# Attention ahead of a mixture of experts: scores made once, normalised exponentials turned by DMA

## The chip, the cores and the metric

The kernel runs on one core of one Trainium2 chip, in one launch. The metric is the device time of that launch in microseconds (us), median of several executions. The engines are named as in the profile: PE is TensorE (matrix products; PEld its weight loads), DVE is VectorE, ACT is ScalarE, POOL is GpSimd, and SP is the engine from whose queue most DMAs are issued.

## What is computed

Four sequences of 576 tokens, eight heads of 64, go through rotary embedding, softmax attention, and then a mixture of eight experts with a Sinkhorn gate. Cut to what matters:

```
q_rot, k_rot = (rotate(q), rotate(k))
scores = scale * np.matmul(q_rot, k_rot.transpose(0, 1, 3, 2))
scores = scores - np.max(scores, axis=-1, keepdims=True)
attn = np.exp(scores)
attn = attn / (np.sum(attn, axis=-1, keepdims=True) + 1e-09)
attn_out = np.matmul(attn, v)
...
x = attn_out.transpose(0, 2, 1, 3).reshape(B * S, H * D)
P = np.exp(x @ w_gate - max)          # then 8 rounds of row and column scaling
for e in range(E):
    out += P[:, e:e+1] * (np.maximum(x @ w1[e], 0.0) @ w2[e])
```

## The kernel before, in words

**Precision.** All is fp32 at the ends. Most products split each operand into a high and a low f16 half ("hl", "hi" and "lo" in the names) and add three products: high x high, high x low, low x high.

**Pairs and units.** Two heads make a pair, 16 pairs in all, four to a sequence. The two heads of a pair stand in the upper and the lower 64 partitions, and their products run side by side on PE. Scores of a pair are made in nine units of 128 x 576 (two heads x 288), one PSUM tile (`s` or `t`, two banks) each.

**The attention before.** The scores are made twice. `s_mm` (L439) makes them with the queries on partitions, only to find each query's maximum (`most`, L462); `m_max` to `m_rows` (L474 to L506) bring the maxima into a row form R. `t_mm` (L508) makes the scores again with the keys on partitions, takes the maxima off by a product with `neg` (L522) and adds the three products (L526); `exps` (L534) writes the exponentials, `e_hi` (L538) and `e_lo` (L541) their f16 halves (tile `eb`). `av_mm` multiplies them with V (L562; in the first three pairs, p < WHOLE, in fp32 with one product, L556), and `sum_mm` (L576) sums the exponentials by products with ones. The sums then go through HBM and back in four steps of small DMAs (`sums_turn`, L586), are inverted on DVE, and `av_norm` and `x_half` (L620, L624) scale the result and split it into `xx`.

**Ahead of a pair** stand the load of Q and K (`load_qk`, L320), their maxima and scales (L294, L364), RoPE (products L386, sums L393) and the split into Z (L295 to L301). V is loaded once a sequence.

**The first expert** (expert 0: `f1_mm` L742, `f2_mm` L765, with ACT's and DVE's halves `hh` L758 and `hl` L763) is cut into five blocks of tokens. Three blocks may start while the attention runs, as soon as their tokens' `xx` is there, and fill PE; two come behind it, beside the gate (L981). After that the other experts run (`experts`, L1422; its products all have L1234).

**What sets the order.** `Plan` (L121) is a list scheduler in the program: each operation has engines, a duration from the table `US`, a due time (`AT`, `SH1`, `RANGES`), buffers that it takes, and what it depends on. Plan walks through time with these numbers and writes each engine's instructions out in that order. On the chip each engine works through its own list in order and waits for semaphores. The table's numbers make the order; they are no measurements.

Of the kernel before, what the change touches and what calls it, by code (L numbers as in the profile page):

```python
# [14 lines left out]
ALU = mybir.AluOpType  # L15
# [36 lines left out]
AT = dict(
    ld=-78.23, mx=-17.61, gm=-23.86, cq=-19.05, ck=-15.91, sc=-18.11, sq=-19.55, sk=-16.41, aq=-17.05, ak=-13.91,
    hq=-24.97, hk=14.53, lq=-34.5, lk=-23.36, mp=-11.68, mh=-11.58, ms=-11.53, ml=-11.48, mt=-10.98, mr=-10.78,
    vh=1.6, vl=-2.58, n0=16.63, d0=4.16, r0=6.82, x0=3.89, h0=4.69, l0=5.19, n1=21.63, d1=9.16, r1=11.82, x1=8.89,
    h1=9.69, l1=10.19,
)
AT_NEW = dict(ldv=-30.41, v0=-8.42, v1=-7.42, v2=-6.42, v3=-5.42, vg=-4.92, vr=-4.82, vp=-4.42)
AV_AT = ((3, 0, 0), (3, 0, 1), (4, 0, 2), (5, 0, 3), (6, 0, 4), (7, 1, 4), (8, 1, 0), (9, 1, 1), (10, 1, 2), (11, 1, 3))

SH1 = dict(
    mx=-0.35, T=0.09, vl=3.02, vh=-8.95, hq=-11.66, eh=-7.16, AVw=0.38, d00=-29.0, d01=-29.0, d02=-29.0, d03=-29.0,
    d10=-29.0, d11=-29.0, d12=-29.0, d13=-29.0, mp=-2.97, mh=-2.97, ms=-2.97, ml=-2.97, mt=-2.97, mr=-2.97,
    lk=-14.85, sc=-2.98, S=-0.04, M=-0.04, ex=-4.13, r0=15.28, r1=15.28, lq=-22.36, Q=-9.6, n0=18.1, n1=18.1,
    hk=-11.04, x0=-1.71, h0=-1.71, l0=-1.71, x1=-1.71, h1=-1.71, l1=-1.71, gm=-46.44, AV=2.25, ck=-0.18, sk=-0.18,
    ak=-0.18, ld=13.84, ldv=-6.05, el=-0.01, cq=-0.22, sq=-0.22, aq=-0.22,
# [3 lines left out]
    s=0.375, mx9=0.68, t=0.5, ex=0.73, eh=0.58, s8=0.42, t4=0.55, av=0.375, av32=1.03, q=0.62, mx=1.26, gm=0.08, tt=0.67, ptt=1.24, sc=0.72, hi=0.68, lo=0.74,  # L70
    ad=0.67, pro=1.37, m1=0.12, m2=0.25, mt=0.12, mr=0.8, n=0.6, d=2.4, dl=5.5, r=0.26, x=0.75, xd=0.37, xh=0.33, xl=0.7, xld=0.37,
# [1515 lines left out]
```

## Time and profile before

| | |
|---|---|
| median of three executions | 1700.3 us (1699.11 to 1700.4) |
| the profiled execution's own time | 1699.66 us |
| its span in the profile | 1697.9 us |
| busy: PE, DVE, ACT, POOL | 1640.5, 1365.7, 1089.8, 686.2 us |
| chain that ended last: PE, DVE, ACT | 85%, 6%, 3% |

A busy share is a mean over stages with different limits, so the stages have to be looked at one by one; and PE being busy does not mean that it runs at its best rate. The program has three stages: attention with most of three blocks of the first expert (to 440 us), gate and the rest of the first expert (to 530), the other experts (to the end).

### The profile page before, as it was taken

The page shows a single profiled execution, that of the slowest core. Times are in us where ns is not written, and L with a number is a line of the kernel's source. Part 1 is how long each engine was busy: PE and PEld are TensorE (multiplying, and loading weights), DVE is VectorE, ACT ScalarE, POOL GpSimd, SP SyncE. Part 2 cuts the span into 40 slices and gives each one's busy share as a digit, 9 for nine tenths or more (in the row PEclk, how much of TensorE's full clock was granted, in tenths as well). Part 3 has the DMA queues.
Part 4 walks back from the last instruction along what each step waited for, and adds up shares of the span by engine and source line. Part 5 has one row for each costly group of instructions (what it writes and reads, how often), then busy time and mean ns, then how long its engine had stood idle before and what let it go on. Part 6 is the DMA issues. An engine that isn't in the chain of part 4 may idle for free.

```text
span 1697.9 us, 39516 instructions
## 1 busy us (share of the span) xinstructions
PE 1640.5 (97%) x16098; PEld 1292.9 (76%) x16098; DVE 1365.7 (80%) x2629; ACT 1089.8 (64%) x2117; POOL 686.2 (40%) x595
## 2 busy tenths in 40 slices
PE   4898999999999999999999999999999999999998
PEld 2454445454455898989898998989898989898987
DVE  7988777752697988888888888888888878888877
ACT  3578777867237666666666666666666666666642
POOL 4466889876243333232323232332323233333310
PEclk8999999999999999999999999999999999999999
DMA  5242222200113464646455655556555555565543
GB/s 219 64 159 71 79 69 78 72 13 19 43 75 112 125 152 123 162 116 160 125 149 130 157 126 150 138 141 144 140 149 138 139 148 150 126 157 128 131 114 94
DMA packets 66543, 203.01 MB, mean 120 GB/s; under 512 B 14660, under 2 KB 19128, under 8 KB 62264
## 3 DMA queue, kind: packets, MB, share of 16 engines
q1 hardware_dynamic: 47640, 139.13, 24.2%
q0 software_dynamic: 18720, 61.35, 19.7%
q8 instruction: 126, 2.06, 0.5%
q14 instruction: 57, 0.47, 0.1%
HBM read 129.46 MB, written 9.64 MB: 82 GB/s over the span
## 4 chain that ended last, share of the span: by engine, by line
PE 85%; DVE 6%; ACT 3%; issue 2%; DMA 2%; POOL 1%; SPq 1%; POOLq 0%; DVEq 0%; ACTq 0%
PE m L1234 66%; PE g L752 4%; PE g L773 4%; PE av L562 3%; PE t L526 2%; PE s L459 2%; PE t L522 2%; DVE mraw L462 1%; PE as L576 1%; DVE Z L297 1%; DMA wraw<-in_w 1%; DVE raw L393 1%; ACT accA L1021 0%; PE av L556 0%; DVE vv L297 0%
## 5 line engine op out<-in xcount | busy, mean ns | idle before, releaser
L1234 PE MATMUL m<-w2h,h 128*128 128x256 f16 x3528 | 627.2, 273 | 3.3 <-DVE accB L1297 1.5
L1234 PEld LDWEIGHTS <-h 128*128 128x128 f16 x5292 | 515.3, 98 | 63.5 <-issue 2.0
L1234 PE MATMUL m<-w2l,h 128*128 128x256 f16 x1764 | 480.8, 273 | 0.0
L1234 PEld LDWEIGHTS <-w1h 128*128 128x128 f16 x3920 | 369.2, 98 | 40.0 <-issue 3.2
L1234 PE MATMUL m<-ts,w1h 128*128 128x256 f16 (+1 forms) x2240 | 347.6, 262 | 2.9 <-ACT m L1257 1.6
L1299 ACT ACTIVATE ev<-m,pp 128x256 f32<-128x256 f32 x468 | 197.5, 467 | 186.3 <-PE m L1234 185.3
L1234 PE MATMUL m<-ts,w1l 128*128 128x256 f16 (+1 forms) x1120 | 284.0, 262 | 0.0
L1234 PE MATMUL m<-xx,w1h 128*128 128x256 f16 (+1 forms) x1680 | 261.4, 262 | 0.0
L1184 POOL TENSOR_TENSOR wraw<-wraw 128x512 f32<-128x512 f32 x112 | 160.8, 1436 | 163.0 <-issue 141.0
L1279 POOL TENSOR_TENSOR h<-u,h 128x512 f16<-128x512 f32 (+1 forms) x70 | 78.2, 1117 | 358.1 <-ACT h L1275 341.0
L1234 PE MATMUL m<-xx,w1l 128*128 128x256 f16 (+1 forms) x840 | 213.1, 262 | 0.0
L1234 PEld LDWEIGHTS <-w1l 128*128 128x128 f16 x1960 | 191.8, 98 | 17.8
L1297 DVE SCALAR_TENSOR_TENSOR ev<-m,pp,ev 128x256 f32<-128x256 f32 x351 | 154.8, 478 | 45.3 <-ACT ev L1299 28.3
L541 POOL TENSOR_TENSOR eb<-e,eb 128x576 f16<-128x576 f32 x117 | 159.4, 1373 | 28.6 <-ACT eb L538 19.8
L462 DVE TENSOR_REDUCE mraw<-s 128x2 f32<-128x576 f32 x140 | 105.4, 753 | 59.4 <-PE s L459 58.3
L1275 ACT ACTIVATE h<-m 128x512 f16<-128x512 f32 (+1 forms) x210 | 120.4, 573 | 44.3 <-PE m L1234 40.8
L1260 DVE TENSOR_TENSOR u<-m,u 128x512 f32<-128x512 f32 (+1 forms) x140 | 88.9, 635 | 54.9 <-PE m L1234 29.2
L1275 ACT ACTIVATE h<-u 128x512 f16<-128x512 f32 (+1 forms) x210 | 122.3, 586 | 14.7 <-DVE u L1286 11.1
L534 ACT ACTIVATE e<-t,ebias,pc 128x576 f32<-128x576 f32 x117 | 97.1, 830 | 38.9 <-PE t L526 37.3
L1257 ACT COPY u<-m 128x512 f32<-128x512 f32 (+1 forms) x140 | 75.8, 542 | 71.5 <-PE m L1234 70.5
L1308 POOL DMA_DIRECT2D accA<-ev x78 | 69.0, 1019 | 126.4 <-ACT ev L1299 108.3
L1308 POOL DMA_DIRECT2D accB<-ev x52 | 45.1, 867 | 181.7 <-ACT h L1275 110.9
(177 smaller groups left out, 2800.2 us busy)
## 6 DMA issues: line engine op xcount, KB each, us to landing
ts<-xd SPq DMA_DIRECT2D x110, 512.0 KB
accA<-ev POOLq DMA_DIRECT2D x78, 512.0 KB, 6.1
wraw<-in_w SPq DMA_DIRECT2D x28, 1024.0 KB
raw<-in_qk SPq DMA_DIRECT2D x32, 576.0 KB
accB<-ev POOLq DMA_DIRECT2D x26, 512.0 KB, 7.2
ts<-xd SPq DMA_DIRECT2D x28, 256.0 KB
accB<-ev POOLq DMA_DIRECT2D x26, 256.0 KB, 3.2
vraw<-in_v SPq DMA_DIRECT2D x4, 1536.0 KB
```

The lines of the kernel that those rows point to most:

```text
L462: dve.reduce_max(o, ps[:, :, 0:HS], axis=AX.X)
L534: act.activation(e32, ps[:, :, 0:HS], AF.Exp, bias=ebias, scale=sc[p][0])
L541: engine[e].tensor_tensor(E[g][:, 1], e32, E[g][:, 0], op=ALU.subtract)
L1184: put(k, "pool", US["ptt"], lambda: pool.tensor_tensor(quad(o), quad(x), quad(y), op=op), deps, uses=[raw])
L1234: pe.matmul(live[bank][:, f_ * width : (f_ + 1) * width], step(x, i, f_), y[:, i], start=first and f_ == 0 and n == 0, stop=n == 5, skip_g ...
L1257: act.copy(live[n], live[src])
L1260: dve.tensor_tensor(live[n], live[x], live[n], **add)
L1275: act.activation(t[:, 0:cols], live[src], func)
L1279: engine[eng].tensor_tensor(l, live[src], h, **sub)
L1297: dve.scalar_tensor_tensor(o, x, s, o, op0=ALU.mult, op1=ALU.add)
L1299: act.activation(o, x, AF.Copy, scale=s)
L1308: pool.dma_start(out=a, in_=ev[th][:, 0:nt], accum_op=ALU.add)
```

## The change

The scores are made once, with the queries on partitions, in five steps a pair (four of 128 queries for each head, one of 64 queries for both heads together). Nine score tiles a pair result, in three PSUM buffers `s`. For each tile DVE takes the negated maximum (`m_max`); ACT makes the bias from it and the exponential in place, with the row's sum (`e_exp`); DVE inverts the sum (`e_inv`); ACT writes the normalised high half (`e_hi`), DVE the low half (`e_lo`), into one of six tiles `et`. SP then turns the tile by a DMA transposition (`e_turn`) into `ET`, where the keys are on partitions, and `av_mm` multiplies with V once five transpositions of a half are there. `ET` is held once for each half of the queries. The products with ones, the maxima's turn, the second score pass and the sums' way through HBM are gone; `x_half` reads PSUM and writes `xx`. RoPE's sums, the scaling of Q, K, V and of the first expert's weights and their low halves move to POOL (`choice`). For the first eight pairs (`SOLO`) the two heads' scores are separate steps. The V blocks shrink from six to five. The tables of due times are new, and RANGES is empty.

The diff, cut (before and after):

```diff
+def choice(pool_us, dve_us):
+    return (("pool", US[pool_us]), ("none", 0.0))[:1] + ((("dve", US[dve_us]),) if BOTH else ())
...
+    def s_mm(n, ps, js):
+        p, i = divmod(n, 5)
+        zz = Z[p]
+        for j in js[:1] if i == TAIL else js:
+            ps[j] = ps_s.tile([P, 2, 512], F32, tag="s", name="s")
+        for x, y in ((0, 2), (1, 2), (0, 3)):
+            for kh in range(2):
+                for j in js:
...
+                    pe.matmul(o, q, zz[r, y, QH[kh]], start=(x, y) == (0, 2), stop=(x, y) == (0, 3))
+    def m_max(ps, b):
+        b.append(small.tile([P, 1], F32, tag="nm", bufs=4, name="nm"))
+        dve.tensor_reduce(b[0], ps[:, :, 0:HS], axis=AX.XY, op=ALU.max, negate=True)
+    def e_exp(p, ps, b):
+        c = small.tile([P, 1], F32, tag="nb", bufs=4, name="nb")
+        act.activation(c, b[0], AF.Copy, bias=E_TOP * math.log(2.0), scale=sc[p][0])
+        b.append(small.tile([P, 1], F32, tag="es", bufs=4, name="es"))
+        e = ps[:, :, 0:HS]
+        act.activation(e, e, AF.Exp, bias=c, scale=sc[p][0], accum_out=b[1])
+    def e_inv(b):
...
+        dve.tensor_scalar(t, b[1], 2.0**-N_TOP, 1e-9 * 2.0 ** (E_TOP - N_TOP), op0=ALU.mult, op1=ALU.add)
...
+        dve.reciprocal(b[2], t)
+    def e_hi(n, ps, b):
+        act.activation(ets[n % NEB][:, 0, 0:S].rearrange("p (a b) -> p a b", a=2), ps[:, :, 0:HS], AF.Copy, scale=b[2])
+    def e_lo(n, ps, b):
+        h, l = (ets[n % NEB][:, x, 0:S].rearrange("p (a b) -> p a b", a=2) for x in range(2))
+        stt_lo(l, ps[:, :, 0:HS], b[2], h)
+    def e_turn(n):
+        p, u = divmod(n, 9)
+        x = ets[n % NEB].rearrange("p n a -> p (n a)")
+        if u == 4:
+            for j, r in enumerate(HEADS):
+                sp.dma_start_transpose(out=ET[:, j, :, 256:320], in_=x[r])
         else:
+            qh, k = divmod(u - (u > 4), 4)
+            at = qh * 320 + k // 2 * P
+            sp.dma_start_transpose(out=ET[:, k % 2, :, at : at + P], in_=x)
...
     def av_mm(p, qh, jt):
+        if jt == 0:
+            avp[p, qh] = ps_g.tile([P, 512], F32, tag="g", name="g")[:, 0:HS]
+        po = avp[p, qh]
+        e = ET[:, :, :, QH[qh]]
         vh, vl = vhl[p]
         for x, n in ((vh, 0), (vl, 0), (vh, 1)):
             for j, r in enumerate(HEADS):
                 pe.matmul(
+                    po[r], x[:, j, jt, :], e[:, j, 5 * n + jt, :], start=jt == 0 and x is vh and n == 0, stop=jt == 4 and n == 1,
                 )
...
+            act.activation(hi, avp[p, qh], AF.Copy, scale=2.0 ** -(N_TOP + 12))
...
+            dve.scalar_tensor_tensor(lo, avp.pop((p, qh)), 2.0 ** -(N_TOP + 12), hi, op0=ALU.mult, op1=ALU.subtract)
...
-        raw=2, Z=3, R=2, S=1, T=1, AV=1, G=2, e32=3, E=EB, vraw=1, vhl=2, xs=4, ss=2, s9=4, rs=2, hA=1, hB=1, mb=2, raw0=1, pc=4, mraw=2,
+        raw=2, Z=ZB, S=3, G=2, E=NEB, ET0=1, ET1=1, vraw=1, vhl=2, hA=1, hB=1, raw0=1, pc=4,
...
+                add("z" + x, choice("ts", "tsd"), 0, lambda e, t=t: z_scale(p, t, e), ["a" + x, "sc"], uses=[rw])
+                add("c" + x, choice("pro", "tt"), 0, lambda e, t=t: rope_mult(e, p, 0, t), ["mx"], uses=[rw])
+                add("s" + x, choice("pro", "tt"), 0, lambda e, t=t: rope_mult(e, p, 1, t), ["ld"], uses=[rw])
+                add("a" + x, choice("ad_p", "ad"), 0, lambda e, t=t: rope_add(p, t, e), ["c" + x, "s" + x], uses=[rw])
...
+                    [f"TR.{9 * p + u}" for u in (range(5) if qh == 0 else range(4, 9))] + [f"vl.{p}"] + ([done] if done else []),
+                allocs=[a] if jt == 0 else [], uses=([] if jt == 0 else [a]) + [et, ("vhl", p)],
```

How the order moves, at two places. The first is DVE's list in the middle of the attention, before (`mraw` is the score maxima, `t_5251` the inverted sums, `mt` and `mm` the turn of maxima, `Z` the low half of Q or K):

```order
L616 TENSOR_REDUCE t_5251<-s_5184 64x9
L618 RECIPROCAL t_5251<-t_5251 64x9
L462 TENSOR_REDUCE mraw<-s 128x2
L466 COPY mt<-mraw 64x1
L467 COPY mraw<-mraw 64x1
L468 COPY mraw<-mt 64x1
L477 TENSOR_REDUCE mm<-mraw 128x9
L297 SCALAR_TENSOR_TENSOR Z<-raw,s,Z 128x576
```

and in the changed program (`et_100` is an exponentials' low half, `hl` the first expert's, `nm` a maximum, `et` and `ei` the sum and its inverse, `e` and `inv` the scales of a later pair):

```order
L285 SCALAR_TENSOR_TENSOR et_100<-s,ei,et_100 128x576
L635 SCALAR_TENSOR_TENSOR hl<-g,hh 128x512
L285 SCALAR_TENSOR_TENSOR et_101<-s,ei,et_101 128x576
L447 TENSOR_REDUCE nm<-s 128x1 x2
L458 TENSOR_SCALAR et<-es 128x1
L460 RECIPROCAL ei<-et 128x1
L272 TENSOR_SCALAR e<-g 128x2
L276 TENSOR_SCALAR inv<-e 128x1 x2
```

Each score tile is now read by DVE twice, for its maximum and for its low half, with the inverse between, and the turn of the maxima and the residues of Q and K are no longer in the list.

The second place is SP's list, before (`raw` is Q and K of a later pair, `sd`, `s`, `si`, `rs` the four steps of the sums through HBM):

```order
L323 DMA raw<-in_qk 128x1152 x2
L594 DMA sd_4499<-ss 1x288 x4
L599 DMA s_4547<-sd_4499 64x9 x2
L603 DMA si_4607<-t_4594 64x9
L609 DMA rs<-si_4607 64x288 x2
```

and in the changed program (`ET` is the turned exponentials, the numbered `et` the six tiles in turn):

```order
L475 DMA_TRANSPOSE ET<-et_102 128x10x64 x2
L479 DMA_TRANSPOSE ET<-et_103 128x10x128
L479 DMA_TRANSPOSE ET<-et_98 128x10x128
L306 DMA raw<-in_qk 128x1152 x2
L479 DMA_TRANSPOSE ET<-et_99 128x10x128
L479 DMA_TRANSPOSE ET<-et_100 128x10x128
```

The loads of Q and K now stand between transpositions, each of which waits for DVE's low half.

## Rows read from the trace of the kernel before

**Rows 1.** Busy us (count) by stretch: PE, PEld, DVE, ACT, POOL, clock, DMA share, GB/s.

```profile
0.00:40.00 40.00, 17.07 (x142) 8.76 (x142) 31.12 (x60) 10.36 (x19) 15.63 (x26) 0.83 0.63 232
40.00:140.00 100.00, 86.47 (x978) 47.39 (x979) 89.78 (x182) 65.96 (x118) 57.68 (x47) 0.97 0.34 110
140.00:220.00 80.00, 72.18 (x863) 37.49 (x862) 63.05 (x119) 63.22 (x112) 61.10 (x49) 0.98 0.19 63
220.00:340.00 120.00, 117.75 (x1389) 61.02 (x1387) 87.02 (x163) 92.55 (x157) 105.75 (x84) 1.00 0.24 76
340.00:440.00 100.00, 100.00 (x1096) 49.36 (x1095) 37.82 (x77) 66.04 (x115) 66.44 (x61) 1.00 0.10 27
440.00:530.00 90.00, 88.90 (x469) 45.89 (x466) 82.11 (x159) 33.64 (x63) 40.11 (x29) 1.00 0.14 53
530.00:1698.00 1168.00, 1158.18 (x11171) 1042.95 (x11168) 974.81 (x1874) 757.99 (x1538) 339.45 (x304) 1.00 0.54 138
```

**Rows 2.** Chain of waits, 360 to 441 us: start, us on the chain, what.

```profile
360.31 0.73 PE as L576 x20
361.04 0.23 PE t L522 x2
361.26 0.37 PE t L526 x6
...
366.74 0.86 PE av L562 x12
...
420.61 18.24 PE g L752 x84
...
440.31 0.22 DVE lg L657
```

**Rows 3.** Groups by line and shape, 0 to 480 us: busy, mean ns | idle before.

```profile
L556 PE MATMUL av<-eb,vv 128*64 128x288 f32 x120 | 21.1, 430 | 1.5 <-ACT x L583 1.3
```

**Rows 4.** The same view, and at the end one line's own view: prices of instructions.

```profile
L462 DVE TENSOR_REDUCE mraw<-s 128x2 f32<-128x576 f32 x140 | 105.4, 753 | 59.4 <-PE s L459 58.3
L534 ACT ACTIVATE e<-t,ebias,pc 128x576 f32<-128x576 f32 x117 | 97.1, 830 | 38.9 <-PE t L526 37.3 <-POOL x L622 0.3
L386 POOL TENSOR_TENSOR raw<-raw,trig 128x576 f32<-128x576 f32 x61 | 93.1, 1541 | 35.1 <-DMA raw<-in_qk 24.8 <-ACT Z L301 5.7 <-ACT eb L534 1.9
L301 ACT ACTIVATE Z<-raw,s 128x576 f16<-128x576 f32 x32 | 24.6, 771 | 22.3 <-DVE raw L393 12.4 <-DMA raw<-in_qk 8.4 <-PE t L526 1.5
L294 DVE TENSOR_REDUCE pmx<-raw 128x2 bf16<-128x1152 f32 x16 | 21.5, 1342 | 4.9 <-DMA raw<-in_qk 4.9
L763 DVE SCALAR_TENSOR_TENSOR hl<-g,hh 128x512 f16<-128x512 f32 x29 | 19.9, 688 | 20.6 <-ACT hh L758 20.5
L758 ACT ACTIVATE hh<-g 128x512 f16<-128x512 f32 x29 | 17.2, 595 | 26.7 <-PE g L752 26.6
L288 DVE TENSOR_SCALAR inv<-e 128x1 f32<-128x1 f32 x40 | 4.7, 150 | 0.8
...
L1013 ACT ACTIVATE ec<-inv x15: 285/287/305, 490.3 to 1587.7; 128x1 f32<-128x1 f32 x15
```

**Rows 5.** Instructions in order of time: start, us, what, idle before and its end.

```profile
491.85 0.36 ACT L758 ACTIVATE hh<-g 128x256 f16<-128x256 f32 x1
...
492.25 0.42 DVE L763 SCALAR_TENSOR_TENSOR hl<-g,hh 128x256 f16<-128x256 f32 x1 [0.72 <-ACT hh L758]
```

**Rows 6.** DMA queue 1 (packets, MB, share) 16 to 30 and 380 to 420; chain.

```profile
q1 hardware_dynamic: 1008, 4.85, 91.4%
...
q1 hardware_dynamic: 1792, 0.64, 6.7%
...
183.53 1.86 DMA s<-sd
```

**Rows 7.** PE by stretch: busy us (count), granted clock, DMA share, GB/s.

```profile
24.00:28.00 4.00, 0.37 (x2) 0.60 1.01 369
...
132.00:136.00 4.00, 2.75 (x26) 0.75 0.17 13
```

More of the change, by code (lines that the diff above doesn't have):

```diff
@@ L41 @@
 E0_IN = 3
-WHOLE = 3
-EB = 8
+NEB = 6
+ZB = 3
+SOLO = 8
+TAIL = 2
+ETU = [(0,)] * 4 + [(0, 1)] + [(1,)] * 4
+QT = (0, 128, None, 320, 448)
 E_TOP = 10
-LEAD = 11
-FIRST = (1, 3, 5, 7)
+N_TOP = 14
+BOTH = False
 AT = dict(
[L53 to L56, printed above, removed]
-)
@@ L128, in add @@
     def add(self, name, engines, at, fn, deps=(), allocs=(), uses=(), lock=False):
-        engines = [engines] if isinstance(engines[0], str) else list(engines)
+        flex = not isinstance(engines[0], str)
+        engines = list(engines) if flex else [engines]
         n = len(self.ops)
@@ L156, in run @@
             k, n = (o[0].split(".") + [""])[0:2]
-            shape.append("ends" if k in ENDS and int(n) % 9 == ENDS[k] else SHAPE.get(k, "whole"))
+            shape.append("ends" if k in ENDS and int(n) % ENDN == ENDS[k] else SHAPE.get(k, "whole"))
         held, ready = {}, {e: set() for e in LATENCY}
@@ L167, in may @@
         def may(n):
+            more = {}
             for tag, _ in ops[n][5]:
-                h, b = held.get(tag, []), self.bufs.get(tag)
-                if b is not None and len(h) >= b and wanted[h[-b]] > 0:
+                h, b, k = held.get(tag, []), self.bufs.get(tag), more.get(tag, 0)
+                more[tag] = k + 1
+                if b is not None and len(h) >= b - k and wanted[h[k - b]] > 0:
                     return False
@@ L456, in s_mm @@
-        for n_, (x, y) in enumerate(((0, 2), (1, 2), (0, 3))):
-            for qc, kh, po in parts:
-                for j, r in enumerate(HEADS):
-                    pe.matmul(po[j], zz[r, x, qc], zz[r, y, QH[kh]], start=n_ == 0, stop=n_ == 2)
-        def most():
-            dve.reduce_max(o, ps[:, :, 0:HS], axis=AX.X)
-            if u == 8:
-                m = mraw[p][:, 1, 8:9]
-                t = small.tile([P, 1], F32, tag="mt", name="mt")
-                dve.tensor_copy(t[0:64], m[64:P])
-                dve.tensor_copy(m[64:P], m[0:64])
-                dve.tensor_copy(m[0:64], t[0:64])
@@ L545, in av_mm @@
-    def av_mm(p, qh, jt):
-        first, last = (0, 4) if qh == 0 else (4, 3)
-        if jt == first:
-            avp[p, qh] = [ps_a.tile([P, 512], F32, tag=t, name=t)[:, 0:HS] for t in ("av", "as")]
-        po, pz = avp[p, qh]
-        e = E[9 * p + (4 if jt == 4 else 5 * qh + jt)]
-        if p < WHOLE:
-            for o, x in ((po, vhl[p][0]), (pz, None)):
-                for j, r in enumerate(HEADS):
-                    a = x[:, j, jt + qh * (jt == 4), :] if x is not None else ones[:, 0:64] if jt < 4 else pick[:, j ^ qh, :]
-                    pe.matmul(o[r], a, e[:, j if jt < 4 else qh, :], start=jt == first, stop=jt == last)
-            return
+        x = ets[n % NEB].rearrange("p n a -> p (n a)")
@@ L562, in av_mm @@
                 pe.matmul(
-                    po[r], x[:, j, jt + qh * (jt == 4), :], e[:, n, j if jt < 4 else qh, :],
-                    start=jt == first and x is vh and n == 0, stop=jt == last and n == 1,
-                )
-    def sum_mm(p, qh):
-        pz = avp[p, qh][1]
-        first, last = (0, 4) if qh == 0 else (4, 3)
-        for jt in (0, 1, 2, 3, 4) if qh == 0 else (4, 0, 1, 2, 3):
-            e = E[9 * p + (4 if jt == 4 else 5 * qh + jt)]
-            for n in range(2):
-                for j in range(2):
-                    r = slice(64 * n + 32 * j, 64 * n + 32 * j + 32)
-                    one = one16[:, 0:32] if jt < 4 else pick16[:, j ^ qh, :]
-                    pe.matmul(pz[r], one, e[:, n, j if jt < 4 else qh, :], start=jt == first, stop=jt == last)
@@ L812, in top_ops @@
         return f"ta.{key}", g
+    before = []
     def pair_ops(p):
         b, c = divmod(p, KC)
-        at = {k: 9 * p + t - (40 if p == 0 and k in ("mp", "mh", "ms", "ml", "mt", "mr") else 0) for k, t in AT.items()}
-        lead = LEAD if p else 50
+        at = {k: 9 * p + t for k, t in AT.items()}
         def add(k, e, us, fn, deps=(), **kw):
@@ L1475, in rel @@
         nonlocal ps_1, ps_h, accq, stg, strm, tmp, hB
-        for x in (att, ps_t, ps_s, ps_a):
+        for x in (att, ps_s):
             x.release()
```

407 lines of the change are left out of this document (128 added, 279 removed), and 7 rows, old and new, of the table RANGES.

## The prediction

> **What bounds the kernel now.** I read the stages first: busy time by stretch [rows 1], cut at the copy of the last logits, which the chain of waits has at 440.31 + 0.22 = 440.5 us [rows 2], and at 530, where the first expert's work ends. From 530 us on PE is busy 1158 of 1168 us [rows 1]; that stage holds none of the changed lines, and the two programs have the same instructions there in the same order, so it is taken over as it is. From 440 to 530 PE works 88.9 of 90 us on the first expert and the gate, with VectorE at 82.1 [rows 1]. Everything that the change touches lies ahead of 440.5. There no one engine bounds all of it: up to 140 us VectorE is the fuller one (89.8 of 100 from 40 to 140, PE 86.5), from 220 on it is PE (117.8 of 120, then 100.0 of 100), and in the last 100 us VectorE has only 37.8 to do [rows 1]. So taking PE work away pays from 220 on, and only until VectorE, ScalarE or a transfer is late instead.
>
> **What goes from PE.** A unit of the second score pass is 0.23 us for the maxima and 0.37 for the scores [rows 2]; 144 units make 86 us. The sum products are 0.73 us for a half pair [rows 2], 26 of them 19 us. The fp32 products of the first three pairs are 240 matmuls of some 0.17 us (21.1 us for 120) [rows 3], 41 us, and become 30 steps of 0.43 [rows 2], 13. The turn of the maxima is about 4 us. Against it the eight SOLO pairs make the heads' scores one after the other: where a unit with both heads side by side is 0.37 for six matmuls (the same kind as in the second pass) [rows 2], one head alone costs between that and twice as much; I take twice, so 64 units gain 0.37 each, 24 us. Net 86 + 19 + 28 + 4 - 24 = 113 us out of the 393 that PE is busy up to 440 (17.1 + 86.5 + 72.2 + 117.8 + 100.0) [rows 1]. PE keeps about 280 us and stops being the bound.
>
> **What VectorE gets.** Every unit now passes VectorE three times. The maximum is the same reduction over 576 fp32 from PSUM, 0.753 us [rows 4]. The inverse is two one-column instructions of 0.15, the second bounded by the first. The low half moves here from POOL and ScalarE's copy: reading PSUM, subtracting an f16 tile, as in hl, 0.688 for 512 columns, so 0.77 for 576 [rows 4]. That is 144 x (0.753 + 0.31 + 0.77) = 264 us. To it come 16 maxima of Q and K at 1.342 (21), their scales at five small instructions (12), 32 halves of x at 0.45 (from 0.42 for 256 columns [rows 5]; 14), maxima of V and the first expert's weights by the same rate (12 + 10), 23 residues hl (16), and pair 0's preparation with the small reductions (18, at up to 1.4 a piece): 367 us. Before, VectorE had 309 us in this stage (31.1 + 89.8 + 63.1 + 87.0 + 37.8) [rows 1]. **So VectorE carries more, not less**, and is the fullest engine.
>
> The others, for cover: ScalarE per unit has the exponential 0.83, the high half (bounds 0.67 from the 0.595 of hh, 0.77 from Z, which has a scale from a tile) and the one-column bias, between the 0.15 of VectorE's kind and the 0.29 of L1013 [rows 4]; 144 x (1.65 to 1.89) plus 79 us of Z, V, x, weights and first expert: 317 to 351. POOL takes all of RoPE, scaling and residues in SBUF, ten instructions a pair at up to 1.54 [rows 4] and two for V, up to 18 us, some 300 in all. Both lie below VectorE and beside it.
>
> **How full VectorE can be.** The nearest rows are the stretches where it was the fuller engine: 89.8% and 91% [rows 1]. I take 90%: 367/0.90 = 408 us. Ahead of it stand 4.9 us without data (the idle time of L294 [rows 4], the same load as before); behind it a tail in which VectorE waits: transposition 3.8 (below), the second half's five products 2.2, two x halves 0.9, logits and their copy 1.5, so 8.4. The mark falls at 4.9 + 408 + 8.4 = 421, against 440.5: **-19.5 us**. What follows the mark is nearly the old 90 us: behind the last product with V there stand 24 matmuls of the first expert's third block (before: 3 behind the logits), at 18.24/84 = 0.217 us [rows 2] 4.6 us more. Nothing there becomes shorter, since PE has no pause in it. The sum is -14.9 us on the profiled execution's own 1699.66: 1684.8. That execution lies 0.6 us under the median of 1700.3, which I leave out.
>
> **What is moved and waits.** On SP the chain of small transfers for the sums goes, and 160 transpositions come in their place. Each waits for the low half on VectorE, and SP issues in order: queued behind it stand the loads of Q, K and V for later pairs, for which POOL's RoPE waits, and the next transpositions. On PE the products with V wait for five transpositions each; queued behind them on PE are the scores of the next units, for which the maxima on VectorE wait. ET is held once per half, so a late product also holds the next pair's transpositions, and the six et tiles then hold ScalarE's high half. A late transposition thus stops every engine of the loop.
>
> **The price of a transposition** is in no row. It moves 128 x 1280 f16, 328 KB. From below: at the 4.85 MB in 14 us of the loads, 0.94 us [rows 6]. Next: as 1280 rows of 256 bytes, 80 on each of 16 engines, at the price of a small packet (6.7% of 16 x 40 us over 1792 packets, 24 ns [rows 6]) 1.9 us. From above: written in pieces of 32 bytes, 640 an engine, 15.4 us. I take 1.9, since those packets are the nearest in size, and 1.86 more until it lands, as a small transfer does [rows 6]: 3.8. A pair then needs 9 x 1.9 + 3.4 (its 1.18 MB of Q and K) + 1.0 (its share of V) = 21.5 us of DMA, against 408/16 = 25.5 of VectorE: hidden, with a margin that ends at 2.35 us a transposition.
>
> **Rivals.**
> *The transpositions set the pace (slower).* Place: the DMA engines and SP's queue. It decides from 2.35 us a transposition on. For: the margin is thin, and every price is borrowed. Against: the engines stood at 10 to 34% in the stage after 40 us [rows 1]. At twice my price, 3.8 us, a pair takes 38.6 us: 16 x 38.6 + 13.3 = 631, 190 + 4.6 more than before, 1894; at 2.8 us 29.6 a pair, 1750.
> *The transpositions go in small pieces (slower by far).* The same place, at the upper end of 15.4 us: 9 x 15.4 + 4.4 = 143 us a pair, 2300 for the stage, 3570. For: nothing in the trace has this kind of transfer. Against: no transfer of whole rows was ever near it. [...]
> *The loop of three score tiles (slower).* A unit holds one of three PSUM tiles from its scores until its low half. For two units made together the tile is free for the next after scores 0.74, maximum 0.75, two exponentials with bias 2 x 1.04, a high half 0.67 and a low half 0.77: 5.0, with five handovers of about 0.05 (492.25 after 491.85 + 0.36) [rows 5] 5.3; a group of three 7.0. Three groups of two and one of three make 22.9 us a pair, under 25.5, so the loop is beside the rest. If VectorE's other work (some 6 us a pair) falls into the loop and not into its gaps, a pair takes 28.9: 16 x 28.9 + 13.3 = 476, +35 + 4.6, 1740. It decides once VectorE's share falls below 86.8%. For: over the whole stage it was 70% before. Against: it was at 90% where it was needed.
> *The loop fits (faster).* At 23 us a pair, VectorE near 100%: 381, 1645. For: most other work of VectorE has pairs of slack. Against: no row shows it above 91% for long.
> [...]
>
> **How the numbers follow.** Forecast, VectorE between 87% and 93%: 0.40, own range 1672 to 1699, likeliest 1685. Loop fits, 1640 to 1672: 0.12. Loop in series, 1699 to 1766 (at 75%): 0.24. Transpositions as the pace, 1750 to 1900: 0.16, half of it under 1790 (3.1 us each). Small pieces: 0.04. Clock: 0.04. A measurement tells 0.2%, 3.4 us, from no change: of the forecast 0.04 and of the loop in series 0.04 lie within, so faster 0.48, same 0.08, slower 0.44. The range 1650 to 1790 leaves out some 0.04 below and 0.16 above.
>
> **What would show it.** In the profile after: VectorE about 367 us busy and 87 to 93% full between 5 and 413 us, the logits' copy at 421, a pair every 25.5 us; transpositions landing within 4 us of issue and DMA engines near 85%; PE about 65% with its pauses ended by VectorE's low half; the first matmul of the second stage some 15 us earlier. Wrong if PE's products with V wait for DMA most of the time (transpositions), if VectorE's idle time is ended by ScalarE and the scores at less than 87% (loop), or if the granted clock stays near 0.5.

## The result, and the profile after

The changed kernel takes 1722.2 us (median of 4 runs, 1720.8 to 1726.8) against 1699.7 for the kernel before in the same comparison: **slower by 22.5 us**, where 1685 was forecast. The ratio, which goes by the means, is 1.0142, 95% interval 1.0117 to 1.0166, or 20 to 28 us. The time lies within the stated range, near the 1740 of the rival "loop of three score tiles"; the sign is wrong. The profiled execution was the longest of the four, 1726.8 us with a span of 1725.0, so what is read in its trace adds up to some 27 us and not to 22.5. All times come from fast runs, and the one execution of scores_one_pass that took 5465 us, the profiled one, is left out, so that kernel has no trace to read.

The copy of the last logits starts at 461.6 us instead of 440.3 [rows 2], and the second stage begins at 556.8 instead of 529.4: in this execution 21.3 us are lost ahead of the logits and 6 behind them. The stretches of the changed kernel; the columns are those of [rows 1]: window, length, busy us (count) of PE, PEld, DVE, ACT and POOL, granted clock, DMA share, GB/s:

```profile
0.00:40.00 40.00, 15.80 (x82) 7.83 (x82) 30.87 (x66) 21.30 (x44) 24.54 (x29) 1.00 0.85 253
40.00:140.00 100.00, 73.35 (x463) 40.67 (x463) 74.79 (x188) 72.86 (x160) 88.91 (x63) 0.70 0.85 177
140.00:220.00 80.00, 57.39 (x440) 32.57 (x437) 65.27 (x156) 61.95 (x139) 73.02 (x52) 0.73 1.02 214
220.00:340.00 120.00, 88.95 (x666) 44.61 (x668) 86.56 (x211) 86.06 (x191) 104.84 (x74) 0.80 0.76 155
340.00:440.00 100.00, 87.80 (x724) 44.52 (x720) 69.39 (x159) 73.73 (x164) 17.85 (x13) 0.98 0.69 110
440.00:462.00 22.00, 21.04 (x192) 11.12 (x187) 12.33 (x26) 11.13 (x24) 2.37 (x4) 1.00 0.74 143
```

Read it against [rows 1]. PE is indeed no longer full from 220 to 340 us (89.0 of 120 instead of 117.8), but neither VectorE nor ScalarE is full in its place: VectorE stands at 69 to 82% in every stretch from 40 to 440 us, ScalarE about as high. The fullest are the transfers and POOL: the DMA share rose from 0.34 and 0.19 to 0.85 and 1.02, and POOL is at 87 to 91% from 40 to 340 us. The granted clock is 0.70 to 0.80 there, where it was 0.97 to 1.00.

The costliest groups from 20 to 460 us (line, engine, operation, shapes, count | busy us, mean ns | idle time before them and what ended it), to be read beside [rows 4]:

```profile
L454 ACT ACTIVATE s<-s,nb,pc 128x576 f32<-128x576 f32 x141 | 113.4, 804 | 4.7
L285 DVE SCALAR_TENSOR_TENSOR et<-s,ei,et 128x576 f16<-128x576 f32 x143 | 113.2, 812 | 15.0 <-ACT et L463 14.6
L447 DVE TENSOR_REDUCE nm<-s 128x1 f32<-128x576 f32 x141 | 102.2, 752 | 43.4 <-PE s L443 42.5
L463 ACT ACTIVATE et<-s,ei 128x576 f16<-128x576 f32 x142 | 100.4, 738 | 9.1 <-DMA ET<-et 5.1 <-DVE ei L460 1.2 <-issue 1.2
...
L385 POOL TENSOR_SCALAR raw<-raw,s 128x576 f32<-128x576 f32 x30 | 51.6, 1724 | 3.2 <-DVE pc L350 1.2
...
L451 ACT ACTIVATE nb<-nm,pc 128x1 f32<-128x1 f32 x141 | 40.7, 289 | 77.1 <-DVE nm L447 76.7
...
L454 ACT ACTIVATION_READ_ACCUMULATOR s<-s,nb,pc 128x1 f32 x141 | 27.0, 191 | 0.0
```

The prices of the unit are close to the forecast ones (maximum 0.752, low half 0.812, high half 0.738, exponential 0.804 us). Two things were not foreseen: behind every exponential that collects its sum there is an accumulator read of 0.191 us, 27 us in all, and POOL's scaling costs 1.724 us.

What the engines waited for from 20 to 460 us (total us, times, longest):

```profile
ACT nb L451 <- DVE nm L447: 76.7, 55, 6.4
PEld L443 <- DVE et L285: 57.8, 46, 3.7
...
PE s L443 <- DVE et L285: 42.7, 35, 3.5
DVE nm L447 <- PE s L443: 42.5, 51, 4.6
DVE et L458 <- ACT s L454: 38.2, 59, 2.2
...
PE g L490 <- DMA ET<-et: 11.8, 11, 4.0
```

These rows close a circle. VectorE's maxima wait for scores (42.5 us), the scores wait for a low half on VectorE that frees their tile (PE 42.7 us), ScalarE waits for maxima (76.7), VectorE's inverse waits for ScalarE's exponential (38.2). Of the 42.7 us of PE, 37.5 lie ahead of 340 us (12.0 from 20 to 140, 10.0 to 220, 15.5 to 340). Here is one turn of the circle, two units, at full clock (start, us, engine, instruction, idle before it):

```profile
400.49 0.91 PE L443 MATMUL s<-Z 64*128 64x288 f16 x12
...
401.44 1.42 DVE L447 TENSOR_REDUCE nm<-s 128x1 f32<-128x576 f32 x2
...
402.23 0.29 ACT L451 ACTIVATE nb<-nm,pc 128x1 f32<-128x1 f32 x1 [1.84 <-DVE nm L447]
...
402.56 0.80 ACT L454 ACTIVATE s<-s,nb,pc 128x576 f32<-128x576 f32 x1
...
403.29 0.19 ACT L454 ACTIVATION_READ_ACCUMULATOR s<-s,nb,pc 128x1 f32 x1
...
403.69 0.80 ACT L454 ACTIVATE s<-s,nb,pc 128x576 f32<-128x576 f32 x1
...
404.52 0.73 ACT L463 ACTIVATE et<-s,ei 128x576 f16<-128x576 f32 x1
...
405.28 0.82 DVE L285 SCALAR_TENSOR_TENSOR et<-s,ei,et 128x576 f16<-128x576 f32 x1 [0.28 <-ACT et L463]
...
405.66 0.38 PE L645 MATMUL g<-wh,hl 128*128 128x512 f16 x1
...
405.97 1.09 PE L443 MATMUL s<-Z 64*128 64x288 f16 x12
```

From scores to scores it is 405.97 - 400.49 = 5.48 us for two units; the rival's estimate, from [rows 2, 4, 5], was 5.3. The next turn, of three units, takes from 405.97 to 413.43, 7.46; the estimate was 7.0. That these agree so well is in part luck: from 401.33 to 406.04 PE works without a pause through 21 matmuls of the first expert (L645, the last is shown), so here its own queue makes the turn as long as the loop does.

Ahead of 340 us PE does stand and wait. A turn there (start, us, engine, instruction, idle before it):

```profile
272.40 1.20 PE L443 MATMUL s<-Z 64*128 64x288 f16 x12
...
274.24 1.41 DVE L447 TENSOR_REDUCE nm<-s 128x1 f32<-128x576 f32 x2
...
274.47 0.72 ACT L415 CAST vv<-vraw 128x640 f16<-128x640 f32 x1 [1.04 <-POOL vraw L420]
...
276.53 0.29 ACT L451 ACTIVATE nb<-nm,pc 128x1 f32<-128x1 f32 x1
...
279.58 0.82 DVE L285 SCALAR_TENSOR_TENSOR et<-s,ei,et 128x576 f16<-128x576 f32 x1 [0.28 <-ACT et L463]
...
280.46 0.91 PE L443 MATMUL s<-Z 64*128 64x288 f16 x11 [3.10 <-DVE et L285]
```

PE waits 3.10 us for the low half, and the turn takes 8.06 us (one matmul of the next scores ran at 277.06, into the tile that was free). The rows also show how POOL gets into the loop: the first maximum is there at 275.0, but in ScalarE's queue casts of V and of the first expert's weights stand ahead of its bias, one of them held for 1.04 us by POOL, and the bias starts only at 276.53. Over the whole stage the first maximum is at 13.6 us and the last at 447.3: 27.1 us a pair, between the rival's 22.9 and 28.9.

### The profile page after: what moved, and what is told of

It reads as the page before. It is cut to its first block, busy times and chain, and to the rows that moved or that the text cites. A ratio compares the mean times of both kernels' runs of the same rounds, so it can differ in the third digit from the quotient of the medians.

```text
span 1725.0 us, 36197 instructions
## 1 busy us (share of the span) xinstructions
PE 1595.5 (92%) x14206; PEld 1271.9 (74%) x14206; DVE 1400.3 (81%) x2834; ACT 1119.5 (65%) x2320; POOL 693.6 (40%) x564
## 4 chain that ended last, share of the span: by engine, by line
PE 70%; DVE 2%; ACT 1%; issue 1%; POOLq 0%; DVEq 0%
PE m L1096 65%; PE g L645 3%; PE g L624 2%; ACT accA L883 0%; DVE prob L868 0%; DVE prob L859 0%; DVE hl L635 0%; ACT h L1137 0%; ACT accB L883 0%; DVE cs L866 0%; DVE accB L1159 0%; DVE u L1148 0%; PE g L490 0%; DVE h L1141 0%; DVE ts L916 0%
## 5 line engine op out<-in xcount | busy, mean ns | idle before, releaser
L443 PE MATMUL s<-Z 64*128 64x288 f16 (+1 forms) x960 | 139.1, 361 | 65.3 <-DVE et L285 42.7
L443 PEld LDWEIGHTS <-Z 64*128 64x128 f16 (+1 forms) x960 | 70.4, 117 | 144.5 <-DVE et L285 60.6
L447 DVE TENSOR_REDUCE nm<-s 128x1 f32<-128x576 f32 x144 | 104.4, 752 | 44.2 <-PE s L443 43.4
L1122 DVE TENSOR_TENSOR u<-m,u 128x512 f32<-128x512 f32 (+1 forms) x140 | 88.9, 635 | 55.0 <-PE m L1096 29.2
L285 DVE SCALAR_TENSOR_TENSOR et<-s,ei,et 128x576 f16<-128x576 f32 x144 | 114.0, 812 | 15.2 <-ACT et L463 14.8
```

What stands on the lines that cost most here:

```text
L285: dve.scalar_tensor_tensor(lo, x, s, hi, op0=ALU.mult, op1=ALU.subtract)
L443: pe.matmul(o, q, zz[r, y, QH[kh]], start=(x, y) == (0, 2), stop=(x, y) == (0, 3))
L447: dve.tensor_reduce(b[0], ps[:, :, 0:HS], axis=AX.XY, op=ALU.max, negate=True)
L1122: dve.tensor_tensor(live[n], live[x], live[n], **add)
```

## The experiments

The ratios are to the kernel before. "Against the changed kernel" is the excess over the kernel before in the same comparison, less the changed kernel's 22.5 us, by medians (for scores_one_pass of the three executions that count). Each such difference carries the interval of its own run and that of the changed kernel, together some 5 us either way, so +0.5, -3.0 and -3.3 can't be told from nothing.

| kernel | ratio, 95% interval | against the changed kernel, us |
|---|---|---|
| no_turns | 1.0081 (1.0066 to 1.0096) | -8.4 |
| no_normalise | 1.0072 (1.0057 to 1.0087) | -11.2 |
| scores_one_pass | 1.0055 (1.0036 to 1.0073) | -13.1 |
| no_pool_scaling | 1.0106 (1.0089 to 1.0123) | -3.3 |
| three_left_out | 0.9885 (0.9871 to 0.9900) | -42.1 |
| three_one_pass | 0.9753 (0.9738 to 0.9767) | -64.7 |
| bias_twice | 1.0309 (1.0292 to 1.0327) | +31.3 |
| more_pool | 1.0269 (1.0253 to 1.0284) | +22.8 |
| more_turns | 1.0542 (1.0527 to 1.0558) | +69.7 |
| turns_apart | 1.0269 (1.0253 to 1.0284) | +24.1 |
| two_tiles | 1.0681 (1.0665 to 1.0697) | +94.2 |
| replanned | 1.0227 (1.0209 to 1.0245) | +15.7 |
| exp_to_sbuf | 1.0538 (1.0522 to 1.0553) | +67.6 |
| exp_to_sbuf_no_turns | 1.0419 (1.0401 to 1.0436) | +48.5 |
| bias_on_vector | 1.0130 (1.0107 to 1.0153) | +0.5 |
| lean | 1.0115 (1.0098 to 1.0131) | -3.0 |
| lean_no_turns | 1.0049 (1.0030 to 1.0068) | -13.2 |
| lean_no_pool_scaling | 1.0067 (1.0052 to 1.0082) | -10.8 |

The theory to begin with was the rival itself: the loop of three score tiles sets the pace. Against it stood the transpositions, and POOL.

### Freeing the tile earlier, with and without transpositions

```diff
-NEB = 6
+NEB = 5
+NXB = 3
...
+    exs = [att.tile([P, 2, HS], F32, name=f"ex{i}") for i in range(NXB)]
...
-        act.activation(e, e, AF.Exp, bias=c, scale=sc[p][0], accum_out=b[1])
+        act.activation(exs[m % NXB], e, AF.Exp, bias=c, scale=sc[p][0], accum_out=b[1])
```

> Here the exponential writes its 128x576 fp32 into one of three tiles in SBUF instead of back into the score tile, and the high and low half read it there, so a score tile is free for the next scores once the exponential is done (et has five tiles instead of six to make room). Loop of three score tiles: in the changed kernel two units made together take 5.5 us from their scores (400.5 us) to the next (406.0); without the inverse, the high and the low half in the hold (about 2.2 us of it) the loop is shorter than VectorE's own work, 341 us for 16 pairs, so VectorE at about 90% sets a pair at 23.7 us against 27; the logits' copy at some 400 instead of 461.6 and the time 1645 to 1685 us. Transpositions (DMA engines 82% busy between 20 and 460 us): nothing of theirs changes, so 1715 to 1730. POOL (90% busy from 60 to 340 us): gain only behind 340 us, 1705 to 1722.

> Both edits at once: the exponential into SBUF, and only the first pair's transpositions. If the loop was the only bound, this gives what the exponential into SBUF gives, within 5 us. If the transpositions (22 us of DMA a pair) are the next bound once the loop is out of the way, this is faster than that by 10 to 30 us, 1630 to 1660.

In both runs the two halves also read `exs` instead of the score tile. All theories missed: 1788.9 and 1769.8 us. The edit brought more with it than the freed tile: there are five tiles `et` instead of six, the planner, which sees the new tiles, made another order, and the low half became dear. First the low half in SBUF from 40 to 140 us and from 440 to 470 (groups, as above), then the busy times of the same two stretches (POOL's is the fifth):

```profile
L286 DVE SCALAR_TENSOR_TENSOR et<-ex,ei,et 128x576 f16<-128x576 f32 x29 | 35.7, 1236 | 4.1 <-ACT et L465 4.0
...
L286 DVE SCALAR_TENSOR_TENSOR et<-ex,ei,et 128x576 f16<-128x576 f32 x13 | 10.6, 816 | 2.3 <-ACT et L465 2.3
```

```profile
40.00:140.00 100.00, 65.27 (x420) 37.69 (x421) 80.00 (x179) 65.77 (x144) 87.96 (x56) 0.81 0.68 150
...
440.00:470.00 30.00, 22.21 (x186) 12.19 (x185) 21.62 (x49) 22.11 (x50) 1.42 (x1) 0.83 1.04 185
```

Beside a busy POOL it takes 1.236 us, beside an idle one 0.816; the changed kernel's low half, which reads the score tile in PSUM, has a mean of 0.812 from 40 to 140 us, with POOL 89% busy. So neither run says anything about the loop.

### Leaving out, one at a time

no_turns issues only pair 0's transpositions; no_normalise drops the sum and the inverse and uses a constant; scores_one_pass keeps one of three passes; no_pool_scaling drops POOL's multiplications, here z_scale and in the same way v_x and w0_x. three_left_out is the first, second and fourth together, three_one_pass all four:

```diff
 def e_turn(n):
...
+        if p > 0:
+            return
...
 def e_exp(p, ps, b):
...
-        act.activation(e, e, AF.Exp, bias=c, scale=sc[p][0], accum_out=b[1])
+        act.activation(e, e, AF.Exp, bias=c, scale=sc[p][0])
...
 def s_mm(n, ps, js):
...
-        for x, y in ((0, 2), (1, 2), (0, 3)):
+        for x, y in ((0, 2),):
...
 def z_scale(p, t, e):
+        return
```

> Only the first pair's nine transpositions are issued; the products of all later pairs read what these left in ET, so the transposition of 15 pairs is left out, and with it the wait for it and its traffic. Order of all other instructions as in the changed kernel. Loop of three score tiles: only the waits for ET (about 12 us on PE) and for loads (14 us on POOL) go, most of them beside the loop: 1700 to 1722 us. Transpositions as the pace: a pair falls from 27 to at most VectorE's 23.7 us, 1640 to 1675.

> The exponential doesn't collect its sum, the inverse isn't made, and both halves take the constant 1/16 in place of it: normalisation is left out, the order of everything else stays. Off ScalarE go 144 accumulator reads of 0.19 us (27 us), off VectorE 144 x 0.31 (45 us). Loop of three score tiles: a pair of units loses two reads and about one inverse of its 5.5 us, some 0.5 to 0.7, so 4.5 groups x 16 pairs give 36 to 50 us back: 1670 to 1690. Transpositions or POOL as the pace: 1710 to 1722.

> Of the three passes of every score tile only the first is left (high half of Q by high half of K): 8 of 12 matmuls of a unit for both heads are left out, nothing else changes, no engine but PE has less to do, and PE isn't full. Loop of three score tiles: the scores stand at the head of every turn, 0.91 us of 5.5 at full clock (400 us) and 1.6 at the low clock (250 us); two thirds of that go, 0.6 to 1.1 us in 4.5 turns a pair, so 43 to 79 us where the loop alone decides, and half of it if it decides half the time: 1640 to 1700. POOL as the pace from 220 to 340 us: no gain there, 1700 to 1712. Transpositions as the pace: 1715 to 1722. If the granted clock falls further because PE does less, the products with V and the first expert give some of it back.

> POOL's multiplications by the scale are left out (Q and K 30 x 1.72, V 16 x 1.89, the first expert's weights 16 x 1.57 us: 107 of its 304 us); the order of the rest stays. POOL as the pace between 220 and 340 us, where pairs take 28 to 31 us and POOL is 87% busy: those five pairs fall to 25 or 26, and the time to 1695 to 1707. Loop of three score tiles or transpositions alone: 1718 to 1724.

> Three ablations at once: transpositions of all pairs but the first, normalisation, and POOL's scaling. Alone the first two gave 9 and 12 us against the changed kernel. If each limit holds in a stretch of its own, the gains add up: some 21 us and what POOL gives, 1685 to 1702. If they stand one close behind the other (what one gives the next takes), together they give clearly more than their sum, below 1680. If the loop of scores, maximum, exponential and halves is all that counts, no more than the 12 of normalisation and a few: 1700 to 1712.

> The three ablations (transpositions of all pairs but the first, normalisation, POOL's scaling) and one pass of the scores instead of three, together: what the last gives when the others are out of the way. With all of them in place it gave 13 us. If the loop is what is left (its chain shows scores for 32% from 20 to 140 us), the scores' two thirds return more than those 13: 25 to 45 of the 1679, 1634 to 1654. If PE's work on the first expert (62% of its chain behind 340 us) has become the bound, 5 to 15 us: 1664 to 1674.

Transpositions as the only pace would have given 47 us or more and gave 8; POOL 15 to 27 and gave 3. That speaks for the loop. But the loop as the only pace should have given 36 to 50 for the normalisation and at least 22 for the scores, and gave 11 and 13. **No single limit holds the pair.** The three together give 42.1 where their sum is 22.9, so part of what one gives back the next takes. (The sum holds the changed kernel's uncertainty three times, some 10 us in the comparison.) With them out of the way the scores' two thirds give 22.6 (64.7 less 42.1) instead of 13.1, just under the loop's lower bound of 25. Two stretches of three_left_out (columns as above):

```profile
140.00:220.00 80.00, 61.83 (x510) 34.48 (x509) 65.36 (x116) 60.42 (x118) 55.80 (x42) 0.86 0.23 85
...
340.00:440.00 100.00, 96.04 (x695) 47.84 (x694) 63.86 (x123) 51.68 (x100) 12.34 (x13) 0.99 0.02 6
```

In the last of them PE is busy 96 of 100 us. The mean time of a pair in us, from the starts of the maxima in the traces (each ninth maximum begins a pair, the first is pair 0):

```
                 pairs 1-7   pairs 8-12
changed kernel     27.1        29.1
no_turns           25.7        28.3
no_normalise       26.0        27.9
no_pool_scaling    26.3        28.5
three_left_out     22.9        25.8
two_tiles          32.7        34.2
```

Up to the start of pair 13 the three alone come 13.4, 14.1 and 8.8 us earlier than the changed kernel, 36.3 in all, and three_left_out 47.6. These are single executions, that of the changed kernel the longest of its four. So the three together give more than their sum here too, but by 11 us, not by the 19 of the medians: how much more is uncertain.

The clock moves with it. PE's stretch up to the start of pair 13 holds the same 1893 matmuls in both kernels; the changed one, then three_left_out (columns as above):

```profile
0.00:373.90 373.90, 263.07 (x1893) 139.57 (x1893) 280.55 (x674) 267.31 (x586) 306.36 (x225) 0.79 0.84 179
...
0.00:326.30 326.30, 236.55 (x1893) 129.71 (x1893) 242.30 (x440) 243.38 (x469) 201.59 (x163) 0.87 0.31 100
```

With the three left out PE stands for 90 us instead of 111, the granted clock is 0.87 instead of 0.79, and the same matmuls keep PE busy for 26.5 us less. No run separates this from what the omissions give by themselves.

### Adding, one at a time

An omission can be taken back by the next limit. An addition has no next limit to hide behind; what hides it is slack, so it shows how much slack there is.

bias_twice makes the bias twice, and more_pool adds a product at the end of z_scale:

```diff
+        for _ in range(2):
             act.activation(c, b[0], AF.Copy, bias=E_TOP * math.log(2.0), scale=sc[p][0])
...
+        rope_mult(e, p, 1, t)
```

more_turns and turns_apart, in e_turn:

```diff
+            for _ in range(1 + (u in (1, 7))):
                 sp.dma_start_transpose(out=ET[:, k % 2, :, at : at + P], in_=x)
```

```diff
             sp.dma_start_transpose(out=ET[:, k % 2, :, at : at + P], in_=x)
+            if u in (1, 7):
+                sp.dma_start_transpose(out=spare[u == 7], in_=x)
```

> Each unit's one-column bias on ScalarE is computed twice, one instruction of 0.29 us more per unit, ahead of the exponential: 42 us of ScalarE in all, which is busy 319 of 440 us. A turn of two units waits for both, so the loop of score tiles is longer by up to 0.58 of 5.5 us. Loop as the pace: +30 to +42, 1752 to 1764. Transpositions or POOL as the pace: the longer loop hides beside them, at most +10, 1732.

> Two of a pair's nine blocks (units 1 and 7) are transposed twice into the same place, 32 more transpositions, whose second copy changes nothing in the result: at 1.48 us of SP's queue each 47 us, and about 2 us of the DMA engines, 64. Transpositions as the pace: +47 to +64, 1769 to 1786. Loop as the pace with the transpositions beside it (DMA engines 82% busy): +0 to +15, up to 1737.

> POOL multiplies a half that is no longer needed once more by the rotary table, two 128x576 products a pair from pair 1 on: 30 x 1.40 = 42 us more on POOL, off every data path but the release of that load buffer. POOL as the pace from 60 to 340 us: +30 to +42, 1752 to 1764. Loop as the pace: 0 to +8, up to 1730.

> Units 1 and 7 of each pair are transposed once more as in the run with doubled transpositions, but into a tile of their own, so that SP doesn't wait for the first copy to land; 32 more transpositions. Transfers at their limit: +47 (SP's 1.48 us each) to +64 (2 us of the DMA engines each), 1769 to 1786, as before. Loop as the pace: those 67 us came of SP standing for some 2 us until the copy before had landed, and 0 to +20 remain, 1722 to 1742.

The longer bias costs 31 of 42 us, as the loop has it. But POOL's 42 us cost 23, nearly three times what the loop alone allows, and the transpositions cost 70. Those 70 are mostly the experiment's own: the second copy goes to the place of the first, so SP waits until the first has landed, and all that is queued behind it waits too. SP's waits for landings of ET in more_turns from 20 to 500 us, which the changed kernel doesn't have (total us, times, longest):

```profile
SPq L480 <- DMA ET<-et: 73.7, 31, 4.3
```

Into a place of their own (`spare`, one tile for both units) the same 32 cost 24 us, half of SP's 47 and a little over the 20 that the loop alone allows. What the products with V waited for ET, in more_turns and in turns_apart (11.8 in the changed kernel):

```profile
PE g L491 <- DMA ET<-et: 45.2, 23, 7.9
```

```profile
PE g L493 <- DMA ET<-et: 34.9, 18, 8.2
```

So neither ScalarE, POOL nor the transfers have much slack at 27 us a pair, though none of them is the pace alone.

### The tiles, the order, and a leaner turn

two_tiles (with S=2 in the plan's buffers), and replanned:

```diff
-    ps_s = mkpool("ps_s", 3, space=PSUM)
+    ps_s = mkpool("ps_s", 2, space=PSUM)
```

```diff
+US.update(ts=1.72,tsv=1.89,tsw=1.57,pro=1.4,ad_p=1.4,ptt=1.28,plv=1.4,plw=1.16,ex=1.28,eh=0.74,el=0.81,M=0.75,ei=0.31,TR=3.6)
```

bias_on_vector moves the bias from e_exp to m_max; lean also makes the inverse in one instruction:

```diff
-        act.activation(c, b[0], AF.Copy, bias=E_TOP * math.log(2.0), scale=sc[p][0])
+        dve.tensor_scalar(c, b[0], sc[p][0], E_TOP * math.log(2.0), op0=ALU.mult, op1=ALU.add)
```

```diff
-N_TOP = 14
+N_TOP = 0
...
-        dve.tensor_scalar(t, b[1], 2.0**-N_TOP, 1e-9 * 2.0 ** (E_TOP - N_TOP), op0=ALU.mult, op1=ALU.add)
...
-        dve.reciprocal(b[2], t)
+        dve.reciprocal(b[2], b[1])
```

> Two score tiles instead of three, order planned anew. A pair of 27 us with nine units in three tiles means that a tile is taken 9 us for each unit, of which the unit's own steps are 5.2. If the number of tiles is the bound, a tile's 9 us stay and a pair takes 40: +213, 1935. If the order of the in-order queues sets the turn (two units go through it together, the third tile is used by half of the turns), a pair takes 27 to 30: 1722 to 1770.

> The changed kernel with the planner's prices put at what the trace shows (POOL's scaling 1.72, 1.89 and 1.57 us for 0.95, 1.05 and 0.85; exponential with bias and accumulator read 1.28 for 0.93; high half 0.74 for 0.56; low half 0.81 for 0.76; transposition 3.6 for 3.4); all instructions are the same, only their order moves. If the order made for wrong prices costs time (in-order queues held by instructions that aren't ready), 1695 to 1715; if the loop's length alone decides, 1715 to 1730.

> The exponential's bias is made on VectorE right behind the maximum (a one-column instruction of 0.15 us as in the inverse) instead of on ScalarE (0.29 us); order else the same, nothing left out. Loop as the pace: 42 us leave ScalarE, at the 0.7 us per us that the doubled bias cost some -29, and 22 us come onto VectorE, +5 to +15: 1698 to 1712. If something beside the loop is the pace: 1718 to 1726.

> As bias_on_vector, and the inverse is one reciprocal of the sum instead of two instructions (no factor 2^14 and no 1e-9 in it; the factor is taken out of the scale behind the product with V too): 144 x 0.15 us less on VectorE, and as much less between the exponential and the high half. Loop as the pace: 4 to 12 us below bias_on_vector, 1688 to 1706, so about level with the kernel before; otherwise no difference to bias_on_vector.

> The lean kernel without the transpositions of all pairs but the first (left out, as before). Leaving them out gave 9 us in the changed kernel and leanness 3. If the gains only add up, 1710 (1707 to 1713), and the turn's length doesn't count. If the transpositions took back what the shorter turn gave, the two together give more: 1690 to 1702.

> The lean kernel without POOL's scaling (left out, as before). Alone that gave 4 us. If POOL took back what the shorter turn gave: 1698 to 1708. If it didn't: 1712 to 1718.

One tile fewer costs 94 us, more than the order alone would (up to 48) and less than tiles alone (213). In two_tiles, 20 to 440 us, PE waited for low halves more than twice as long as with three (total us, times, longest):

```profile
PEld L443 <- DVE et L285: 131.2, 72, 5.4
PE s L443 <- DVE et L285: 100.3, 55, 5.1
```

So the number of tiles matters, together with the order in which the queues serve them. The order planned with the measured prices is slower by 16 us, outside both ranges. So putting the prices right doesn't help; it also shows that the order alone moves the time by as much, and no other order was tried.

bias_on_vector and lean came out 11 and 13 us above their ranges. A turn of lean shows one reason (instructions in order of time):

```profile
395.90 0.91 PE L443 MATMUL s<-Z 64*128 64x288 f16 x12
...
396.84 0.76 DVE L447 TENSOR_REDUCE nm<-s 128x1 f32<-128x576 f32 x1 [0.37 <-PE s L443]
...
397.63 0.21 DVE L449 TENSOR_SCALAR nb<-nm,pc 128x1 f32<-128x1 f32 x1
...
400.44 0.82 DVE L285 SCALAR_TENSOR_TENSOR et<-s,ei,et 128x576 f16<-128x576 f32 x1 [0.47 <-ACT et L463]
...
401.07 0.38 PE L645 MATMUL g<-wh,hl 128*128 128x512 f16 x1
...
401.38 1.98 PE L443 MATMUL s<-Z 64*128 64x288 f16 x24
```

The bias on VectorE is 0.21 us, not 0.15. From the maximum to the low half the turn is 3.60 us instead of 3.84 (401.44 to 405.28 in the changed kernel): 0.24 saved, some 17 us over 72 turns at best, where 29 were expected of the bias alone. From scores to scores it is 401.38 - 395.90 = 5.48, just as before: PE works through matmuls of the first expert's second product that stand in its queue ahead of the next scores (the last here at 401.07), so the shorter turn gives nothing there. The transpositions didn't take it back: leaving them out gives 10.2 in lean (13.2 less 3.0) and 8.4 in the changed kernel, and 1707 us lies where the gains only add up. Whether POOL took part of it isn't shown: without its scaling, leanness gives 7.5 (10.8 less 3.3) instead of 3.0, a difference within the noise, and 1709.6 us lies between the two ranges. Neither bias_on_vector nor lean beats the kernel before.

## Why the prediction was wrong, point by point

**VectorE at 90%: the step that failed.** Its load was, if anything, put too high: 339 us busy up to 462 where 367 were forecast. The units' 264 came out at 263.6 (114.0, 104.4, 21.6 and 23.6 us); what else it has was put 28 us too high. But it was 339 of 449 us full, 76%, between the 4.6 us without data and the tail. The 90% came from two stretches of the kernel before [rows 1]. One of them, the 91%, was misread: it is the stretch from 440 to 530 us (82.1 of 90), in which PE was the fuller engine at 88.9. In the other, units had a short way back from VectorE to PE: the maximum alone freed the score tile, and PE waited little for it (before, 20 to 440 us):

```profile
PE s L459 <- DVE mraw L462: 9.1, 13, 2.0
```

In the changed kernel a tile passes PE, VectorE, ScalarE, VectorE, ScalarE, VectorE and only then goes back to PE, which waits 42.7 us for it, and VectorE waits for ScalarE twice in each turn. The stretches of before could not show how full an engine gets when its input depends on its own output over so long a way. The prediction had this as a rival and gave it 0.24; its condition, under 86.8%, came true.

**The rival's size.** 22.9 us a pair with nothing else in the loop, 28.9 with all of VectorE's other work in it; 27.1 was measured. As a mechanism it is borne out where the loop was made worse (two_tiles, bias_twice); as the sole cause it isn't (the omissions), and the two runs that shorten it (bias_on_vector, lean) gave nothing that can be told from noise.

**The transpositions.** 3.8 us from issue to landing were forecast, and 3.6 measured; beside [rows 6], the view of the tile ET (minimum, median and longest ns on SP's queue) and the page's part on DMA issues (count, median us to landing):

```profile
L479 SPq DMA_TRANSPOSE ET<-et x128: 1252/1484/6334, 19.4 to 453.3; - x128
```

```profile
ET<-et SPq DMA_TRANSPOSE x160, 3.6
```

Ten blocks of 128 x 128 were in SP's queue for 1.48 us (median) and landed 3.6 us after their issue (median). The pieces of 32 bytes behind the rival's 15.4 us were an assumption: they would have been 1.47 million packets, and the whole trace has 243131. The forecast of DMA engines near 85% held from 40 to 140 us, but they stood at 102% from 140 to 220, and "hidden, with a margin" was too kind: leaving out all but the first pair's gives 8.4 us, and 32 more cost 24.

**PE and its clock.** PE was to keep 280 us of work and was busy 344 up to 462, at a granted clock of 0.83 on average (280/0.83 is 337) and of 0.70 to 0.80 from 40 to 340 us, near the 0.75 of [rows 7]. The prediction gave the clock a chance of 0.04 and no term in its sum. PE isn't full before 340 us, but the scores are a part of every turn, and slower matmuls make the turn longer: eleven score matmuls in a row took 1.62 us at 250.03, where 0.50 was granted (249 to 253), and 0.91 at 425.36, where 1.00 was (380 to 440). The clock also moved with the waits: in three_left_out PE stood for less time and was granted 0.87 instead of 0.79 up to pair 13. How much of the 22 us this is stays open: no run changed the clock alone. From 340 us on the first expert's matmuls, which PE does between the scores, fill it (87.8 of 100, and 21.0 of 22 at the end).

**POOL** was put at some 300 us and was busy 311 up to 462, beside the rest as said; but up to 340 us it is 87 to 91% busy, and 42 us more on it cost 23.

**Head and tail** held, the tail by luck. The tail from the last low half (452.9) to the logits' copy (461.6) is 8.7 us where 8.4 was forecast, but by another way: PE did matmuls of the first expert until 457.2 and then the second half's products with V. The end of the chain (start, us, what), beside [rows 2]:

```profile
449.96 7.28 PE g L624 x33
457.24 1.98 PE g L490 x30
```

Behind the mark 6 us were lost where 4.6 were forecast.

**What stays open:** the clock's share, how the 22 us divide among loop, transfers and POOL, since each takes part of what another gives back, and two parts of the change that no run varied: the separate steps of the two heads in the first eight pairs, and the due times that make the order.

## What to carry to other kernels

Before an engine's load is divided by a share of fullness, follow one buffer around: if its release comes back to the engine that starts it, the pace is no better than the turn's length over the number of buffers, with the order of the in-order queues on top, and no engine need be full. Where every engine and the transfers are as full as here from 40 to 340 us (PE 73%, VectorE 76, ScalarE 74, POOL 89, transfers 86), an omission measures too little (8.4, 11.2 and 3.3 us alone, 42.1 together) and an addition shows the missing slack: try both, and several omissions at once. An experiment with an added transfer must not make a queue wait for a landing, or it measures that (69.7 us here, and 24.1 into a place of its own).

## What the runs showed of the hardware

- An activation that collects a sum is followed by an accumulator read of 191 ns on ScalarE.
- POOL's multiplication of 128x576 fp32 by a column takes 1.724 us, more than the product of two such tiles (1.403).
- A VectorE instruction with both inputs in SBUF took 1.236 us beside a POOL 88% busy and 0.816 beside one 5% busy. With one of the inputs in PSUM it took 0.812 beside a POOL 89% busy (40 to 140) and 0.813 beside one 5% busy (380 to 440).
- A transposition of 128x1280 f16 held SP's queue for 1.25 us at least, 1.48 in the median and up to 6.3.
- The granted clock was 0.70 with PE busy 73 of 100 us (40 to 140) and 0.98 with PE busy 88 of 100 (340 to 440). The same 1893 matmuls kept PE busy for 263.1 us at 0.79 and for 236.6 at 0.87.
